# Attention units in another order: the 448- and the 576-column unit of every pair change places

## The chip, the cores and the metric

The kernel runs on one core of one Trainium2 chip. The metric is the device time of one execution in microseconds (us); less is better. TensorE is called PE here, its weight loads PEld, VectorE DVE, ScalarE ACT, GpSimd POOL, and SP is the queue that issues most DMAs.

## The reference

Causal attention with a decay, for 4 batches of 8 heads, 576 tokens and head size 64, and two feed-forward layers behind it (2304 tokens, width 512):

```
scores = scale * q @ k.T                       # per head, 576 x 576
cum    = cumsum(log(clip(f, 1e-4, 1)))
scores = where(causal, -1e9, scores + cum[:, None] - cum[None, :])
attn   = exp(scores - max) / (sum + 1e-9)
x      = attn @ v                              # heads side by side: 2304 x 512
x      = rms_norm(x) * g
x      = (silu(x @ w_gate) * (x @ w_val)) @ w_out    # 512 -> 1536 -> 512
out    = silu(x @ w_in) @ w_out2                     # 512 -> 2048 -> 512
```

## The kernel before

**Units.** The attention runs over 16 pairs of heads (4 batches of 4 pairs). Both heads of a pair sit side by side in 128 partitions. The 576 queries of a pair are cut into nine blocks of 64. Block c, with both heads 128 rows, needs the keys up to its own, (c + 1) * 64 columns; this is a unit of class `Rows` (line 449). So a pair has nine units, of 64 to 576 columns, and `ORDER` (line 33) says in which order they come. All 144 units form one row, and a loop (line 644) walks along it, one step for each unit:

```
if 0 <= s + 1 < N:     units[s + 1].bias()       # POOL
if 0 <= s - TURN < N:  units[s - TURN].turn()    # PE, then ACT or DVE; TURN = 4
if 0 <= s < N:         units[s].scores()         # PE, then DVE
                       units[s].expo()           # ACT
if 0 <= s - USE < N:   units[s - USE].use()      # PE, then ACT; USE = 6
for fn in jobs.pop(s, ()): fn()
```

Position 0 is the first unit of a pair here, position 8 its last. "The turn at position 3" is then the turn of the unit at position 8 of the pair before, since the turn is four steps behind the scores.

**The steps of a unit.** `bias` (line 455) makes the decay row `dt` on POOL; there are six buffers. `scores` (line 463) takes three matmuls (L472: high and low parts) into a PSUM bank of the kind "s", of which there are four, shared in turn with the transposes of the next pair's operands. One DVE instruction (L475) then adds the decay, writes `pr` and takes the extreme `nm`. A bank holds 512 columns, so the unit of 576 columns takes two banks (320 and 256 columns), two L475, and one small DVE instruction more (L482) that joins the two extremes. `expo` (L488) is one exponential on ACT, behind it an instruction that reads the row sum. `turn` (line 491) transposes the probabilities on PE into a bank of the kind "t" (three of them) and moves them to SBUF as `g`. Which engine does that move is said by `ON_ACT = (3, 4, 5, 6, 7, 9, 10, 11)`: unit 6 (448 columns) is moved by ACT, unit 8 (576 columns) by DVE, and unit 8 has one transpose more (L504) with a move of its own, `gl`, on ACT. `use` (L528) multiplies by the values for the whole pair when the step of the pair's last unit comes (`if self.c == ORDER[-1]`).

**Jobs.** During a pair, at fixed positions, the operands of the next pair are made: position 1 loads its decay sums, position 3 transposes its keys (L425, "nk"), position 4 its queries (L425, "nq"), position 5, behind `use`, the tails (L442). Each takes an "s" bank; ACT writes the high part out of it (L273) and DVE the low part (L274), and then the bank is free. At the end of each batch some steps more are there: row sums (L321, L323), the mean of squares (L303, L310), the scale factors (L371, L377, L380).

**Order of the queues.** Each engine works through its own queue in order. The program order above is where the queues start from; the framework's planner orders each queue when the kernel is built, and gives out the banks, by its own idea of when things are ready. While the attention runs, weights of the feed-forward layers are loaded and repacked on ACT (L148) and DVE (L149 to L152). The feed-forward layers (L778) follow.

Of the kernel before, what the change touches and what calls it, by code (L numbers as in the profile page):

```python
# [29 lines left out]

WARM = (12, 1, 2, 5)

ORDER = (0, 1, 7, 2, 6, 3, 5, 4, 8)

TURN = 4
USE = 6
# [26 lines left out]
def block_kernel(ctx: ExitStack, tc: tile.TileContext, q, k, v, f, w_gate, w_val, w_o1, rms_g, w_in, w_o2, ident_d, sel_d, hot_d, out):  # L63
# [150 lines left out]
    def attention():  # L214
        exps, maxima = [], []
        with ExitStack() as st:
# [232 lines left out]
            class Rows:  # L449
# [57 lines left out]
                def use(self):  # L507
                    if self.c == ORDER[-1]:
                        outs = [self.use_group(gi) for gi in range(2)]
                        for out_ in outs:  # L510
                            out_()
# [112 lines left out]
            for n, p in enumerate(pairs):  # L624
                s = n * per
                units += [Rows(p, c) for c in ORDER]
                if n:
# [409 lines left out]
```

## Time and profile before

| | |
|---|---|
| median of 3 runs | 1025.91 us (1025.36 to 1026.23) |
| the profiled execution | 1025.31 us |
| its span, first to last instruction | 1023.5 us |
| busy in the span: PE / PEld / DVE / ACT / POOL | 1011.4 / 847.7 / 761.1 / 566.9 / 401.2 us |
| granted TensorE clock | 1.0 in the whole span (2.4 GHz) |
| attention, to about 216 us | ACT busy 191.58 us, DVE 178.26 us |

A row of a timeline gives start and duration, engine, line, and what is written out of what. Matmuls are pipelined: the duration of one reaches over the start of the next, so that the distance from start to start is what one costs, and a PE that shows as busy may still have room.

### The profile page before, as it was taken

Reading aid. Unit: us, or ns where it says so; the run is one execution under the profiler, and the core shown is the slowest. Engines: PE = TensorE matmul, PEld = TensorE weight load, DVE = VectorE, ACT = ScalarE, POOL = GpSimd, SP = SyncE. Lnnn points to the kernel's source line nnn. Section 1 sums busy time; section 2 is a strip of 40 time slices with the busy share of each in tenths; the row PEclk is TensorE's granted clock in tenths of the full one; section 3 lists DMA queues with packets and bytes.
Section 4 is the critical chain, followed back from the end, with each engine's and each line's share of the span. In section 5 each row is a group of like instructions: output and inputs, shape, how many; then the busy total and the mean of one; then the engine's idle time right before and its main releaser. Section 6 shows DMA issues by size and latency. Waiting matters only on the chain.

```text
span 1023.5 us, 16104 instructions
## 1 busy us (share of the span) xinstructions
PE 1011.4 (99%) x5463; PEld 847.7 (83%) x5463; DVE 761.1 (74%) x1520; ACT 566.9 (55%) x1193; POOL 401.2 (39%) x613
## 2 busy tenths in 40 slices
PE   9999999999999999999999999999999999999998
PEld 7787788878888888888888888888888888888887
DVE  7889887877778797976688768846666696466664
ACT  7998989873444232544544556564444464534441
POOL 8777666511022026331365334435533322222310
PEclk9999999999999999999999999999999999999999
DMA  5764533123544444231334122223322233121102
GB/s 140 193 189 114 126 92 94 27 63 124 185 142 167 159 150 154 73 124 49 106 124 143 64 65 79 83 83 114 113 83 83 83 124 144 42 71 54 52 1 83
DMA packets 114162, 106.40 MB, mean 104 GB/s; under 512 B 62896, under 2 KB 83792, under 8 KB 114080
## 3 DMA queue, kind: packets, MB, share of 16 engines
q1 hardware_dynamic: 112352, 102.23, 32.5%
q10 hardware_dynamic: 1728, 3.15, 1.0%
q8 instruction: 43, 0.70, 0.3%
q14 instruction: 39, 0.32, 0.1%
HBM read 79.59 MB, written 25.76 MB: 103 GB/s over the span
## 4 chain that ended last, share of the span: by engine, by line
PE 77%; DVE 2%; issue 0%; ACT 0%
PE t L778 40%; PE s L778 20%; PE x L778 16%; PE o L528 0%; DVE hl L696 0%; PE s L303 0%; DVE b11l L696 0%; DVE c L912 0%; PE t L497 0%; PE t L528 0%; DVE f L151 0%; DVE ms L342 0%; ACT pr L488 0%; DVE c L152 0%; DVE wl L174 0%
## 5 line engine op out<-in xcount | busy, mean ns | idle before, releaser
L206 POOL TENSOR_TENSOR wol<-c,woh 128x512 fp32r<-128x512 f32 x53 | 78.7, 1491 | 241.8 <-ACT woh L205 218.3
L696 DVE TENSOR_TENSOR hl<-c,hh 128x512 fp32r<-128x512 f32 (+1 forms) x140 | 114.4, 825 | 45.3 <-ACT hh L695 44.4
L167 POOL TENSOR_TENSOR f<-f 128x256 f32<-128x256 f32 x112 | 93.7, 859 | 112.9 <-DMA f<-keptb 51.2
L695 ACT ACTIVATE hh<-c 128x512 fp32r<-128x512 f32 (+1 forms) x140 | 79.7, 582 | 46.3 <-DVE c L912 41.6
L790 ACT ACTIVATE c<-t 128x512 f32<-128x512 f32 x84 | 49.8, 593 | 95.0 <-PE t L778 93.9
L459 POOL TENSOR_SCALAR dt<-ncb,c8t 128x64 f32<-128x64 f32 (+2 forms) x144 | 79.2, 552 | 35.9 <-DVE nm L475 27.5
L488 ACT ACTIVATE pr<-pr,nm 128x192 f32<-128x192 f32 (+3 forms) x144 | 80.2, 558 | 11.6 <-DVE nm L475 8.1
L905 ACT ACTIVATE c<-c 128x512 f32<-128x512 f32 x66 | 41.6, 630 | 80.8 <-DVE c L795 80.8
L475 DVE CUSTOM_DVE_ANT_0 pr<-s,dt 128x256 f32<-128x256 f32 (+7 forms) x160 | 70.1, 450 | 13.4 <-PE t L497 4.8
L193 POOL TENSOR_TENSOR wl<-f,wh 128x1024 fp32r<-128x1024 f32 x12 | 28.8, 2396 | 125.6 <-ACT wh L192 118.9
L497 PE MATMUL t<-ident,pr 128*128 128x128 f32 x384 | 69.2, 279 | 3.7 <-ACT pr L488 2.6
L174 DVE TENSOR_TENSOR wl<-f,wh 128x1024 fp32r<-128x1024 f32 (+1 forms) x48 | 57.7, 1209 | 20.4 <-ACT wh L172 20.2
L795 DVE TENSOR_TENSOR c<-t,c 128x512 f32<-128x512 f32 x60 | 41.1, 687 | 39.4 <-ACT c L790 26.2
L172 ACT ACTIVATE wh<-f 128x1024 fp32r<-128x1024 f32 (+1 forms) x56 | 54.4, 973 | 23.4 <-PE x L778 18.9
L778 PE MATMUL s<-hh,woh 128*128 128x512 f32 (+1 forms) x172 | 64.0, 372 | 0.2 <-DVE xa L959 0.2
L778 PE MATMUL s<-hh,wol 128*128 128x512 f32 (+1 forms) x172 | 64.0, 372 | 0.0
L778 PE MATMUL s<-hl,woh 128*128 128x512 f32 (+1 forms) x172 | 63.9, 372 | 0.0
L977 DVE TENSOR_TENSOR xa<-x,xa 128x512 f32<-128x512 f32 x64 | 43.5, 682 | 25.2 <-PE x L778 25.1
L977 DVE TENSOR_TENSOR xa<-s,xa 128x512 f32<-128x512 f32 (+1 forms) x63 | 42.9, 683 | 25.5 <-PE s L778 25.1
L905 ACT ACTIVATE c<-t 128x512 f32<-128x512 f32 (+1 forms) x74 | 37.9, 512 | 35.9 <-PE t L778 33.8
L148 ACT ACTIVATE f<-st 128x512 f32<-128x512 f32 x42 | 27.8, 668 | 53.6 <-DMA keptb<-f 18.1
L959 DVE TENSOR_TENSOR xa<-s,xa 128x512 f32<-128x512 f32 (+1 forms) x72 | 45.4, 638 | 14.0 <-PE s L778 13.9
(248 smaller groups left out, 3234.1 us busy)
## 6 DMA issues: line engine op xcount, KB each, us to landing
st<-in_moe_w_out_dram SPq DMA_DIRECT2D x28, 512.0 KB, 3.7
st<-in_moe_w_in_dram SPq DMA_DIRECT2D x16, 512.0 KB, 3.8
f<-keptb SPq DMA_DIRECT2D x32, 256.0 KB, 2.6
st<-in_moe_w_gate_dram SPq DMA_DIRECT2D x12, 512.0 KB, 4.2
kepta<-f SPq DMA_DIRECT2D x24, 256.0 KB, 2.3
st<-in_moe_w_val_dram SPq DMA_DIRECT2D x12, 512.0 KB, 4.6
f<-kepta SPq DMA_DIRECT2D x24, 256.0 KB, 2.8
out_dram<-xa SPq DMA_DIRECT2D x17, 256.0 KB, 2.0
```

The lines of the kernel that those rows point to most:

```text
L167: nc.gpsimd.tensor_tensor(out=out_, in0=x, in1=y, op=op)
L174: (nc.gpsimd if plain and i else nc.vector).tensor_tensor(out=lo[i][:, v], in0=f[i][:, v], in1=hi[i][:, v].bitcast(F32), op=ALU.subtract)
L206: nc.gpsimd.tensor_tensor(out=lo, in0=f, in1=hi.bitcast(F32), op=ALU.subtract)
L459: nc.gpsimd.tensor_scalar(out=dt, in0=p.nct[:, 0 if last else D :][:, :n], scalar1=c8t[:, c, p.i : p.i + 1], scalar2=1.0, op0=ALU.add, op1 ...
L475: reduced = nc.vector.tensor_tensor_reduce(out=self.pr[:, ks], in0=sp, in1=self.dt[:, ks], op0=ALU.add, op1=ALU.min, scale=-SCALE, scalar= ...
L488: e = nc.scalar.activation(out=pr, in_=pr, func=AF.Exp, bias=self.nm, scale=-1.0, accum_out=p.batch.sums[:, self.c, p.hp : p.hp + 1])
L497: nc.tensor.transpose(pt[:, jj * P : (jj + 1) * P], keys[:, jj * P : (jj + 1) * P], ident)
L695: nc.scalar.activation(out=hi, in_=src, func=AF.Copy)
L696: nc.vector.tensor_tensor(out=lo, in0=src, in1=hi.bitcast(F32), op=ALU.subtract)
L778: nc.tensor.matmul(ps, lhsT=l, rhs=r, start=start and z == 0, stop=stop and z == len(mms) - 1, skip_group_check=not (start and stop))
L905: act = nc.scalar.activation(out=hf, in_=a, func=AF.Silu)
L977: nc.vector.tensor_tensor(out=a, in0=ps, in1=a, op=ALU.add)
```

## The change

The sixth and the eighth entry of the table are exchanged: unit 8 (576 columns) goes from position 8 to position 4, unit 6 (448 columns) from position 4 to position 8, in all 16 pairs. All else in the text of the kernel stays: `use` comes at the same step, but the last unit ahead of it is now unit 6; and the moves stay with their engines.

```diff
-ORDER = (0, 1, 7, 2, 6, 3, 5, 4, 8)
+ORDER = (0, 1, 7, 2, 8, 3, 5, 4, 6)
```

In columns: before 64, 128, 512, 192, 448, 256, 384, 320, 576; after 64, 128, 512, 192, 576, 256, 384, 320, 448.

## Rows read from the trace of the kernel before

**Rows 1.** Busy time in two stretches: us; PE, PEld, DVE, ACT, POOL (instructions), clock.

```profile
0.00:216.00 216.00, 207.80 (x1621) 171.96 (x1621) 178.26 (x638) 191.58 (x553) 144.15 (x381) 1.00 0.46 116
216.00:1023.50 807.50, 803.61 (x3843) 675.76 (x3843) 582.89 (x883) 375.33 (x641) 257.03 (x232) 1.00 0.31 101
```

**Rows 2.** Waits of PEld (weight loads) to 217 us: total, times, longest.

```profile
PEld t L497 <- ACT pr L488: 8.0, 18, 0.9
```

**Rows 3.** Timeline of PE around the turn at position 3, one pair.

```profile
158.65 0.38 PE L497 MATMUL t<-ident,pr 128*128 128x128 f32 x2
...
160.37 0.39 PE L472 MATMUL s<-op0l,op0h 128*128 128x512 f32 x1
160.60 0.40 PE L472 MATMUL s<-op0h,op0l 128*128 128x512 f32 x1
161.43 0.66 PE L497 MATMUL t<-ident,pr 128*128 128x128 f32 x4 [0.44 <-ACT pr L488]
...
163.97 0.36 PE L472 MATMUL s<-op0h 128*128 128x256 f32 x1
...
169.13 0.60 PE L497 MATMUL t<-ident,pr 128*128 128x128 f32 x4
```

**Rows 4.** The same turn in the first and in the last of the nine pairs where it waits.

```profile
21.53 0.28 PE L472 MATMUL s<-op1l,op1h 128*128 128x192 f32 x1
21.79 0.66 PE L497 MATMUL t<-ident,pr 128*128 128x128 f32 x4
...
186.35 0.25 PE L472 MATMUL s<-op0h 128*128 128x192 f32 x1
186.44 0.28 PE L472 MATMUL s<-op0l,op0h 128*128 128x192 f32 x1
187.03 0.66 PE L497 MATMUL t<-ident,pr 128*128 128x128 f32 x4 [0.32 <-ACT pr L488]
```

**Rows 5.** Timeline of DVE in the stretch of rows 3.

```profile
158.42 0.49 DVE L475 CUSTOM_DVE_ANT_0 pr<-s,dt 128x320 f32<-128x320 f32 x1
...
160.06 0.17 DVE L482 TENSOR_TENSOR nm<-nm 128x1 f32<-128x1 f32 x1
...
162.67 0.69 DVE L280 COPY g<-t 128x512 f32<-128x512 f32 x1
...
164.79 1.28 DVE L274 TENSOR_TENSOR op1l<-s,op1h 128x512 fp32r<-128x512 f32 x2 [0.34 <-ACT op1h L273]
```

**Rows 6.** Timeline of ACT in the same stretch.

```profile
160.18 0.35 ACT L488 ACTIVATE pr<-pr,nm 128x64 f32<-128x64 f32 x1 [0.26 <-DVE nm L475]
...
160.52 0.76 ACT L488 ACTIVATE pr<-pr,nm 128x576 f32<-128x576 f32 x1
161.19 0.19 ACT L488 ACTIVATION_READ_ACCUMULATOR pr<-pr,nm 128x1 f32 x1
```

**Rows 7.** Groups by shape to 270 us: busy us, mean ns.

```profile
L475 DVE CUSTOM_DVE_ANT_0 pr<-s,dt 128x448 f32<-128x448 f32 x16 | 9.9, 619 | 1.8 <-POOL pr L484 0.5 <-ACT pr L488 0.5 <-POOL dt L459 0.4
...
L488 ACT ACTIVATE pr<-pr,nm 128x448 f32<-128x448 f32 x16 | 10.6, 665 | 1.5 <-DVE nm L475 1.5
```

**Rows 8.** Timeline of PE, the second bank of unit 8, first and last of five pairs.

```profile
65.59 0.31 PE L472 MATMUL s<-op0h,op0l 128*128 128x320 f32 x1
66.14 0.35 PE L472 MATMUL s<-op0h 128*128 128x256 f32 x1 [0.24 <-DVE op1l L274]
...
195.93 0.31 PE L472 MATMUL s<-op0h,op0l 128*128 128x320 f32 x1
196.27 0.39 PE L472 MATMUL s<-op0h 128*128 128x256 f32 x1
```

**Rows 9.** Timeline, the unit of 256 columns at position 5 of another pair.

```profile
47.46 0.27 PE L497 MATMUL t<-ident,pr 128*128 128x128 f32 x1
47.53 0.34 DVE L475 CUSTOM_DVE_ANT_0 pr<-s,dt 128x192 f32<-128x192 f32 x1
...
47.94 0.39 PE L472 MATMUL s<-op1h 128*128 128x256 f32 x1 [0.21 <-DVE nm L475]
```

## The prediction

> **What bounds the kernel now.** I read the stretches first: where is PE the limit? Behind 216 us PE is busy 803.6 of 807.5 us, in the attention 207.8 of 216, with ACT at 191.6 and DVE at 178.3 [rows 1]. So the feed-forward part has no room, and the change touches nothing in it: it starts earlier or later by what the attention gains or loses, and no more. In the attention the busy share of PE says little, since durations reach over the next start; there I went by starts. The Trainium skill (Perfetto Trace Analysis, "Identifying the Most-Contended Engine") goes by another row: not matmul busy time, but the share of the weight loads tells how much room TensorE has. By it the estimate of the room would be 216 less 172.0 / 0.837 (the share behind 216 us, 675.8 of 807.5), 10.5 us [rows 1], against 8.2 by matmul busy time; the sum below does not use it.
>
> Second the waits: the largest of the weight loads in the attention is that of turns (L497) for exponentials, 8.0 us in 18 times [rows 2]. Third the timelines, to see which turn that is. In nine of the 16 pairs it is the turn at position 3, that of unit 8 of the pair before. It has the shortest way of all: three units after its own scores, but these are 64, 128 and 512 columns. In the pair shown its scores are issued by 158.65, and the turn could go at 160.60 + 0.23 (the distance of two 512-column matmuls) = 160.83, 2.2 us later. It goes at 161.43: 0.60 us lost [rows 3]. What was late: unit 8 needs two L475 and the joining L482, which stands in DVE's queue behind the small unit and ends at 160.23; then ACT does the exponential of 64 columns first, that of 576 from 160.52, and its row sum is read at 161.38 [rows 5, 6]. The turn follows at once.
>
> By the same subtraction the nine waits are 0.6 three times, 0.5 three times, 0.3 twice and between 0.1 and 0.2 once. In the first pair it is 21.79 - 21.53 = 0.26 less about 0.1 for a matmul of 192 columns (186.44 - 186.35 = 0.09), in the last 187.03 - 186.44 = 0.59 less the same 0.1 [rows 4]. Together 4.1 us. In the other pairs jobs of the batch's end lie between, and nothing waits.
>
> **The change part by part.** No instruction is added or removed: the same matmuls, L475, exponentials, moves and DMAs. What moves is their place.
>
> *Unit 8 leaves the short way.* At position 4 its turn is at position 8, with the units of 256, 384 and 320 columns and `use` between: from 163.97 to the turn at 169.13 in the pair shown, 5.2 us where 2.7 were needed (158.65 to 161.38) [rows 3, 6]. Its wait of 4.1 us in all goes.
>
> *Unit 6 comes onto the short way.* One L475 of 0.62, no L482, an exponential of 0.67 in place of 0.76 [rows 5, 6, 7]. But unit 8's turn is now in the step just ahead of it (position 8), and DVE's copy of 0.69 belongs to that turn [rows 5]. If the copy comes first: L475 of the 320-column unit ends with its read at about 159.0, the copy to 159.6, L475 of unit 6 to 160.2 with the read, the exponential with its row sum (0.67 + 0.19 from 160.52 to 161.38, less the 0.1 for a shorter row: about 0.8) to 160.95. The turn could go at 160.83, so 0.1 us stays. If the copy comes behind, nothing stays. I take 0.1 in nine pairs: 0.9 us back. The bounds are 0 and 0.3 (if ACT again does the 64-column exponential first, 0.35 [rows 6], of which 0.1 lies beside).
>
> *The second bank of 576 columns.* At position 8 it waits in five pairs: 66.14 - 65.59 = 0.55, where a 320-column matmul costs 0.14 (0.23 of rows 3 times 320/512), so 0.41; the last of the five 0.34 - 0.14 = 0.20 [rows 8]. The five make 1.5 us (0.4, 0.4, 0.2, 0.2, 0.2). There unit 6 takes one bank, and the next is asked for a whole unit later: 1.5 us go.
>
> *Banks at positions 4 and 5.* There one bank more is wanted, next to the keys' (position 3) and the queries' (position 4), which are held longest: the keys' is free only when DVE has made the low part, at about 165.4, while the 256-column unit wants a bank at 163.97 [rows 3, 5]. Rows do not show unit 8 there, so I bound it. From below: nothing. The first bank of unit 8 is read as soon as its matmuls end if DVE is not behind; it takes 0.5, and PE's second half (0.12 a matmul by the same scale, three of them) and the queries' transposes lie between, some 0.8. DVE is less behind there, since the copy of 0.69 at 162.67 [rows 5] has left position 3. From above: the wait for the keys' bank, 165.4 - 163.97 = 1.4 us in each of 15 pairs, 21 us. The nearest row is the same unit at the same place, waiting for a DVE instruction that stands behind weight work: 47.94 - 47.46 less 0.03 for a transpose, 0.45 us [rows 9]. Such waits of some 0.45 are there in four pairs already. I take 0.2 us in eight pairs (those in which DVE repacks weights), 1.6 us, because 0.45 is for a DVE that is behind and nothing for one that is not.
>
> *What costs nothing.* The move of unit 6 (ACT) goes to position 3, that of unit 8 (DVE, and ACT's `gl`) to position 8: `use` needs them only two steps later, and ACT's queue there loses `gl` and gains some 0.3 us; the keys' high part comes later by that, under `use`. Without that cover it is in the 21 us above. POOL prepares each `dt` ahead in six buffers, so its 576-column row at another step is covered by the five units before it; without that it would be the 0.1 us by which that row is longer. SP's loads stay at their steps. Of the three "t" banks unit 8 still takes two in one step, and two engines still free them, DVE's copy and ACT's `gl`. The last pair's tail (no later scores to hide behind) I take at nothing, between -0.5 and +0.5: one L475 less, but the copy ahead of it.
>
> Sum: -4.1 - 1.5 + 0.9 + 1.6 = -3.1 us on the profiled execution's 1025.31 (span 1023.5 and 1.8 around it), which stands 0.6 below the median of 1025.91. From the median: **1022.8 us**. The feed-forward part passes it on.
>
> **The rivals.**
> A. *The gain goes to another wait; no change.* ACT is busy 89% of the attention and DVE 83% [rows 1]. In pairs with a batch's end or weight work a PE that comes earlier may only wait for a bank a step later. Against it: the nine waits are caused by an order of queues, not by a lack of engine time, and DVE and ACT stand in that order because unit 8 has more steps than any other [rows 5, 6]. If 4 of the 5.6 us come back so: -1.6 us, 1024.3. 0.26.
> B. *The bank at position 5; slower.* If the 256-column unit gets the keys' bank, or unit 8's L475 stand behind the keys' low part on DVE (0.65 each, half of rows 5's 1.28), it waits 0.65 us in 15 pairs: +9.8 - 5.6 + 0.9 = +5.1, 1031.0. It decides from (5.6 - 0.9) / 15 = 0.3 us a pair. For it: four waits there already [rows 9]. Against it: in rows 8 the wanted bank is not always the one given out longest ago, and in rows 4 the plan has pulled matmuls of the next unit ahead of a late turn; `use` could be pulled ahead likewise. The Trainium skill (the same page, "Optimization Strategy") says that a gap that repeats on the engine that should be full can mean that there is no PSUM for the next tile; rows 8 agree, and by that rule the change carries the gap from position 8 to position 4 or 5 and this rival is what it gives. 0.19.
> C. *The change does all at no cost:* -4.1 - 1.5 - 0.5 (tail) = -6.1, 1019.8: the good end of the forecast.
>
> **How the numbers follow.** Forecast (with C) 0.55, A 0.26, B 0.19. About 0.2%, 2 us, is what a measurement tells from no change. Forecast: faster; A: -1.6 lies inside, as part of the forecast's own spread does, and as part of A's spread lies beyond it. So faster 0.55, same 0.26, slower 0.19. The forecast's own range is 1019.5 to 1024. For 8 in 10 I reach from just under C, 1019.0, into B: the milder half of it, 1030.0.
>
> **What the profile would show.** Right: the L497 of position 3 starts within 0.25 us of the last 512-column matmul, and PEld's wait of turns for exponentials falls from 8.0 to about 4 us; no second bank waits at position 8; the feed-forward part, behind 216 us before, starts some 3 us earlier. A step is wrong if PE waits at position 3 as before (then the copy stands ahead and ACT's order is bad), or if L472 of 256 columns or the second bank of unit 8 waits for DVE L274 or L475 in most pairs (B). The prediction as a whole is wrong if the stretch behind the attention changes its own length by more than 1 us.

## The result, and the profile after

The changed kernel takes 1039.87 us (median of 4 runs, 1039.49 to 1040.61), the kernel before on the same chip 1025.63: 14.2 us more, ratio 1.014 with a 95% interval of 1.0127 to 1.0153. The forecast was 1022.8, in a range from 1019.0 to 1030.0. It went the way of rival B, and further than its price.

The stretches of the kernel after; columns as in [rows 1].

```profile
0.00:230.50 230.50, 214.89 (x1621) 171.84 (x1621) 184.03 (x639) 192.62 (x553) 145.24 (x381) 1.00 0.43 110
230.50:1038.50 808.00, 803.43 (x3843) 675.92 (x3843) 582.37 (x882) 374.52 (x641) 256.43 (x232) 1.00 0.31 100
```

The same 1621 matmuls of the first stretch take 230.5 us in place of 216, with the same weight-load time (171.8 against 172.0): nothing became dearer, there are only more gaps. The second stretch is 808.0 against 807.5 [rows 1]. The whole loss lies in the attention, at a granted clock of 1.00.

The waits of the kernel after, first of PEld to 232 us (the rows that answer to [rows 2]), then one of ACT from 18 to 222 us.

```profile
PEld t L497 <- ACT pr L488: 5.9, 14, 0.8
PEld s L472 <- DVE nm L475: 5.2, 13, 0.8
PEld t L504 <- ACT g L278: 4.7, 6, 1.5
PEld s L425 <- DVE nm L475: 3.2, 6, 0.8
```
```profile
ACT pr L488 <- DVE nm L482: 6.0, 11, 1.3
```

Two rows of the kernel before, from 18 to 222 us:

```profile
PEld s L472 <- DVE nm L475: 3.0, 8, 0.5
ACT pr L488 <- DVE nm L482: 0.7, 2, 0.4
```

Turns wait less for exponentials, 5.9 us where it was 8.0 [rows 2], as forecast in its direction. But scores and operands (L472, L425) wait for DVE to read banks, 8.4 us together where L472 alone had 3.0; unit 8's fifth transpose (L504) waits for ACT's moves; and ACT itself stands 6.0 us in 11 times with unit 8's exponential at the head of its queue, waiting for the joining L482.

One pair shows how these hang together. Position 4 in the kernel after, DVE's timeline:

```profile
134.23 0.49 DVE L475 CUSTOM_DVE_ANT_0 pr<-s,dt 128x320 f32<-128x320 f32 x1 [0.29 <-ACT pr L488]
134.65 0.08 DVE L475 DVE_READ_ACCUMULATOR2_ANT nm<- 128x1 f32 x1
...
135.56 0.69 DVE L274 TENSOR_TENSOR op0l<-s,op0h 128x512 fp32r<-128x512 f32 x1 [0.83 <-ACT op0h L273]
...
136.17 0.41 DVE L475 CUSTOM_DVE_ANT_0 pr<-s,dt 128x256 f32<-128x256 f32 x1
...
136.51 0.29 DVE L280 COPY g<-t 128x128 f32<-128x128 f32 x1
...
136.71 0.19 DVE L482 TENSOR_TENSOR nm<-nm 128x1 f32<-128x1 f32 x1
```

The same stretch on PE, then on ACT:

```profile
134.12 0.28 PE L472 MATMUL s<-op1h,op1l 128*128 128x256 f32 x1
...
135.24 0.66 PE L425 MATMUL s<-ident,nq 128*128 128x128 f32 x4
...
136.40 0.36 PE L472 MATMUL s<-op1h 128*128 128x256 f32 x1 [0.51 <-DVE op0l L274]
```
```profile
134.03 0.58 ACT L278 ACTIVATE g<-t 128x512 f32<-128x512 f32 x1
134.51 0.45 ACT L488 ACTIVATE pr<-pr,nm 128x192 f32<-128x192 f32 x1
134.85 0.19 ACT L488 ACTIVATION_READ_ACCUMULATOR pr<-pr,nm 128x1 f32 x1
134.95 0.58 ACT L273 ACTIVATE op0h<-s 128x512 fp32r<-128x512 f32 x1
135.93 0.59 ACT L273 ACTIVATE op0h<-s 64x512 fp32r<-64x512 f32 x1 [0.40 <-PE s L425]
137.02 0.78 ACT L488 ACTIVATE pr<-pr,nm 128x576 f32<-128x576 f32 x1 [0.50 <-DVE nm L482]
```

Unit 8's second half is in its bank at 134.4. DVE, done with the first half at 134.7, has the low part of the keys (L274) next in its queue. That needs ACT's high part, and ACT comes to it only at 134.95, behind a move and an exponential. So DVE stands for 0.83 us, works 0.6 on the keys, and reads the second half from 136.17: its bank is held some 1.4 us longer than DVE's work on unit 8 asks for. The 256-column unit starts at 136.40, and the row names what it waited for: not unit 8's bank, which is still being read, but the one that L274 lets go, the keys'. The exponential starts at 137.02, 2.6 us behind its scores. In the trace an L274 stands between unit 8's two L475 in 7 of 16 pairs, and in 8 more between them and the join alone; in the kernel before in none, since at position 8 no keys or queries are near.

That pair is not the common case of PE's waits for "s" banks. Position 4 of another pair, DVE, then PE:

```profile
91.42 0.57 DVE L353 SCALAR_TENSOR_TENSOR z<-z,ms 128x5 f32<-128x5 f32 x1
92.03 0.17 DVE L355 SCALAR_TENSOR_TENSOR y<-z,y 128x5 f32<-128x5 f32 x1
92.17 0.36 DVE L475 CUSTOM_DVE_ANT_0 pr<-s,dt 128x192 f32<-128x192 f32 x1
...
93.71 0.69 DVE L274 TENSOR_TENSOR op1l<-s,op1h 128x512 fp32r<-128x512 f32 x1
94.31 0.15 DVE L482 TENSOR_TENSOR nm<-nm 128x1 f32<-128x1 f32 x1
```
```profile
92.59 0.66 PE L425 MATMUL s<-ident,nq 128*128 128x128 f32 x4 [0.55 <-DVE nm L475]
```

Unit 8 has taken two banks, so the queries (L425) wait until the 192-column unit's is read. DVE reads it late, and not for ACT: it is behind with scale factors of the batch's end. The L274 comes after both halves and delays the join alone. Of the 19 waits of L472 and L425 for L475 listed above, 11, together 5.9 of the 8.4 us, end at an L475 that DVE reached late in this way, without a pause, behind steps of a batch's end or the repacking of weights.

What was forecast of position 3 and position 8 came true. PE of the kernel after, the turn at position 3:

```profile
171.35 0.39 PE L472 MATMUL s<-op0l,op0h 128*128 128x512 f32 x1
171.58 0.40 PE L472 MATMUL s<-op0h,op0l 128*128 128x512 f32 x1
171.87 0.66 PE L497 MATMUL t<-ident,pr 128*128 128x128 f32 x4
```

It starts 0.29 behind the last 512-column matmul, 0.06 above what a matmul of that size takes, where it was 0.60 above [rows 3]. The turn at position 8, however, has a gap of its own now; PE, then ACT:

```profile
179.79 0.60 PE L497 MATMUL t<-ident,pr 128*128 128x128 f32 x4
181.68 0.30 PE L504 MATMUL t<-ident,pr 128*64 128x128 f32 x1 [1.30 <-ACT g L278]
```
```profile
181.03 0.60 ACT L278 ACTIVATE g<-t 128x512 f32<-128x512 f32 x1
```

The fifth transpose wants a second "t" bank, and the one that comes free is unit 7's, which ACT moves only at 181.03.

### The profile page after: what moved, and what is told of

Read it like the earlier page. It is cut to its first block, busy times and chain, and to the rows that moved or that the text cites. A ratio compares the mean times of both kernels' runs of the same rounds, so it can differ in the third digit from the quotient of the medians.

```text
span 1038.5 us, 16113 instructions
## 1 busy us (share of the span) xinstructions
PE 1018.3 (98%) x5463; PEld 847.8 (82%) x5463; DVE 766.4 (74%) x1520; ACT 567.1 (55%) x1193; POOL 401.7 (39%) x613
## 4 chain that ended last, share of the span: by engine, by line
PE 83%; ACT 5%; DVE 4%; issue 1%; DMA 1%; POOL 0%; SPq 0%; ACTq 0%; DVEq 0%
PE t L778 39%; PE s L778 20%; PE x L778 16%; PE s L472 2%; ACT pr L488 2%; PE o L528 2%; PE t L497 2%; ACT g L278 1%; DVE pr L475 1%; PE t L528 1%; DMA st<-in_moe_w_in_dram 0%; DVE r L321 0%; PE s L303 0%; PE s L377 0%; ACT op0h L273 0%
## 5 line engine op out<-in xcount | busy, mean ns | idle before, releaser
L696 DVE TENSOR_TENSOR hl<-c,hh 128x512 fp32r<-128x512 f32 (+1 forms) x140 | 116.7, 842 | 45.0 <-ACT hh L695 44.2
L488 ACT ACTIVATE pr<-pr,nm 128x64 f32<-128x64 f32 (+2 forms) x144 | 80.1, 557 | 19.8 <-DVE nm L475 13.1
L475 DVE CUSTOM_DVE_ANT_0 pr<-s,dt 128x256 f32<-128x256 f32 (+7 forms) x160 | 70.4, 449 | 14.8 <-PE t L497 4.9
```

The lines of the kernel that those rows point to most:

```text
L475: reduced = nc.vector.tensor_tensor_reduce(out=self.pr[:, ks], in0=sp, in1=self.dt[:, ks], op0=ALU.add, op1=ALU.min, scale=-SCALE, scalar= ...
L488: e = nc.scalar.activation(out=pr, in_=pr, func=AF.Exp, bias=self.nm, scale=-1.0, accum_out=p.batch.sums[:, self.c, p.hp : p.hp + 1])
L696: nc.vector.tensor_tensor(out=lo, in0=src, in1=hi.bitcast(F32), op=ALU.subtract)
```

## The experiments

Three theories were set against each other as the runs went on. S: five "s" banks are wanted at positions 4 and 5, and there are four. T: at position 8 unit 8 takes two of three "t" banks. Q, later Q': the queues of DVE and ACT are in a worse order; Q' names the place, the keys' L274 within unit 8's DVE steps. Each time is given with its distance from the kernel before in the same series (1025.25 to 1025.54); the changed kernel stands at +14.2.

**The banks, by way of the "o" bank.** This is the one bank of a third kind; only `use`, at position 5, asks for it. L504's target and the second half's target are changed, alone and together, and together in the order of before:

```diff
-pt = bank(pst)                 # fifth transpose of unit 8
+pt = bank(pso)
...
-sp = bank(pss)[:, :w]          # scores
+sp = bank(pso if n > SF and k0 else pss)[:, :w]
```

> The changed order, but the fifth transpose of unit 8 (L504) writes to the 'o' bank, which is idle at that step, in place of a second 't' bank. Theory T (at position 8 unit 8 asks for two of three t banks right behind the turns of units 7 and 2, and PE waits until ACT has moved unit 7): 4.2 us of waits of L504 go and some of the turns behind it, so 1033 to 1035 us. Theory S (the fifth scores bank wanted at positions 4 and 5 is the loss): within 1 us of the changed kernel's 1039.9. Theory Q (the queues of ACT and DVE are in a worse order, banks only show it): no change, 1039 to 1040.

> The changed order, but the second half of unit 8's scores goes to the 'o' bank in place of a second 's' bank, so that positions 4 and 5 ask for as many s banks as before the change. Theory S: the waits of L425 (2.2 us), of the 256-column matmuls and of unit 8's two halves (some 6 us together) go, 1031 to 1034 us. Theory T: 1039 to 1040. Theory Q: 1039 to 1040.

> The changed order with both: second half of unit 8's scores and its fifth transpose in the 'o' bank. If the whole loss is banks (T and S together), 1024 to 1028 us, the time of before or below it. Theory Q: above 1036. T alone 1033 to 1035, S alone 1031 to 1034.

> The order of before with the same two edits. They take away the waits of the second half at position 8 (1.2 to 1.5 us), and nothing else is known to wait for these banks there: 1024.0 to 1025.6 us by S and T alike; Q expects 1025.6.

Fifth transpose: 1038.79 (+13.5). Second half: 1032.80 (+7.5). Both: 1031.89 (+6.6). Control: 1025.55 (+0.2, interval of the ratio 0.9991 to 1.001). T brings 0.8 us and falls as the main cause, although its wait was the longest single gap: with the second "t" bank out of the way the lateness shows elsewhere, PEld's wait of turns for exponentials to 232 us going from 5.9 to 9.3 us. S brings 6.8, about half. Where the rest went is seen in the waits of the run with both, from 18 to 222 us:

```profile
PEld o L528 <- DVE nm L475: 5.6, 10, 1.2
...
ACT pr L488 <- DVE nm L482: 4.2, 7, 1.0
```

Now `use` waits for the "o" bank until DVE has read unit 8's second half, up to 1.2 us: the bank is still read late. That turned the question from how many banks to what DVE does in between.

**Queries and tails one step later.**

```diff
-WHEN = dict(load=-12, k=-6, sums=-8, q=-5, tails=-4)
+WHEN = dict(load=-12, k=-6, sums=-8, q=-4, tails=-3)
```

> The changed order with all banks as they were, but the next pair's queries are transposed one step later (position 5, behind use, in place of position 4) and its tails at position 6, so that only the keys share the s banks with unit 8's two halves and the 256-column unit. Theory S (too many s banks wanted at positions 4 and 5): a gain like that of the second half in the o bank, without its cost to use: 1029 to 1033 us. Theory Q (the order of work on ACT and DVE, whatever the banks): 1039 to 1040, since the same work comes only 4 us later.

> The order of before with queries and tails one step later, the control. S expects next to nothing, since positions 4 and 5 have only some 0.8 us of bank waits to lose: 1024.5 to 1026. If the later step is of use for another reason, it is faster here too, by several us.

> The changed order with queries and tails one step later and unit 8's fifth transpose in the o bank. S with T as the second cause: 2 to 4 us under the run with the later queries alone. S alone, the t banks being only where a late ACT shows: within 1 us of it.

1047.81 (+22.3) in the changed order, 1043.50 (+18.0) in the order of before, 1046.39 (+20.9) with the fifth transpose in the "o" bank. All missed what was expected: the later step costs 18 us by itself, for a reason that I did not follow up, so the runs do not tell S from Q. Only this much: with the queries elsewhere the two orders lie 4.3 us apart, not 14.2.

**The keys' L274 out of unit 8's way.** Keys behind unit 8's scores (k=-5) or one step ahead (k=-7), or unit 8's DVE steps given priority when the queue is planned; and the keys behind the unit of position 4 in the order of before:

```diff
-WHEN = dict(load=-12, k=-6, sums=-8, q=-5, tails=-4)
+WHEN = dict(load=-12, k=-5, sums=-8, q=-5, tails=-4)     # the other run: k=-7
```
```diff
+with tc.high_priority(offset=AHEAD) if n > SF else ExitStack():
     reduced = nc.vector.tensor_tensor_reduce(...)        # L475
...
+with tc.high_priority(offset=AHEAD):
     nc.vector.tensor_tensor(out=nms[0], in0=nms[0], in1=nms[1], op=ALU.min)   # L482
```

> The changed order; the next pair's keys are transposed behind the scores of unit 8 (position 4, ahead of the queries) in place of position 3. Theory Q' (at position 4 DVE's queue has the low part of the keys, L274, which waits for ACT, between unit 8's two L475 or ahead of the joining L482; unit 8's exponential and, behind it on ACT, all moves come late, and the second bank stays held): in this kernel's DVE queue no L274 stands between unit 8's first L475 and its L482 in any pair (in the changed kernel one does in most), so 6 to 12 us of the 14 come back, 1028 to 1034. Theory S (the number of s banks asked for at positions 4 and 5, wherever DVE's queue stands): the same five banks are asked for within the same two steps, so 1038 to 1041.

> The changed order, where unit 8's L475 and L482 have priority over other ready work in the planning of DVE's queue. No L274 stands between the two L475 any more, but one still stands ahead of L482 in 13 of 16 pairs, since L482 is not ready at once. Q': part of it comes back, 2 to 6 us, 1034 to 1038: the bank is free earlier, the exponential is not. If the bank held by the second half is all of it: 1031 to 1034.

> The changed order; the keys one step earlier (position 2, behind the 512-column unit). L274 of the keys then stands behind the 512-column unit's L475, none between unit 8's two, and ahead of L482 mostly a small copy. Q': 1028 to 1034 if ACT makes the high part in time, less if DVE now waits for ACT ahead of the 192-column unit. S: 1036 to 1040 (the keys' bank comes free a little earlier).

> The order of before with the keys behind unit 6 at position 4, the control for the run with the keys behind unit 8. Q' expects little, since unit 6 has one L475 and nothing that L274 could split: 1024.5 to 1027. If keys behind the scores are better or worse for a reason of their own, it shows here.

Keys behind: 1031.38 (+6.1). Priority: 1034.24 (+9.0). Keys earlier: 1037.62 (+12.3). Control: 1026.33 (+1.1). The first is the plain case for Q': the same banks are asked for within the same steps, and 8.1 us come back with DVE reading unit 8 at once. Its DVE, the same place in a pair:

```profile
129.12 0.49 DVE L475 CUSTOM_DVE_ANT_0 pr<-s,dt 128x320 f32<-128x320 f32 x1
...
129.54 0.42 DVE L475 CUSTOM_DVE_ANT_0 pr<-s,dt 128x256 f32<-128x256 f32 x1
...
130.00 0.16 DVE L482 TENSOR_TENSOR nm<-nm 128x1 f32<-128x1 f32 x1
130.84 0.69 DVE L274 TENSOR_TENSOR op0l<-s,op0h 128x512 fp32r<-128x512 f32 x1 [0.68 <-ACT op0h L273]
```

The two halves and the join follow each other (129.12 to 130.16; 134.23 to 136.90 in the changed kernel), and DVE's wait for ACT, still 0.68, comes behind them. Moving the keys also changes the order in which banks are asked for, unit 8's two now ahead of the keys'. The priority edit touches DVE's steps alone; it leaves no L274 between the halves, but one ahead of the join in 13 pairs, and brings 5.3 us. So DVE's queue counts without any change in the requests. Which part of it counts most, the held bank or the late exponential, is not shown. Waits of the keys behind, from 18 to 222 us:

```profile
PEld s L425 <- DVE nm L475: 4.2, 9, 0.9
PEld s L472 <- DVE nm L475: 3.7, 8, 0.8
PEld t L504 <- ACT g L278: 3.0, 6, 1.0
...
ACT pr L488 <- DVE nm L482: 3.3, 5, 1.1
```

The waits for banks that DVE reads are as long as in the changed kernel (7.9 us against 7.7 in this stretch); those for ACT's moves and of ACT for the join are shorter, 3.0 us where it was 4.7 and 3.3 where it was 6.0. That speaks for the late exponential as what this edit gives back, and is no test.

Keys earlier is the run that went against Q': 1.9 us, in the range that S gave. No L274 stands between unit 8's halves there and one ahead of the join in 4 pairs only, so a queue of DVE that is clear around unit 8 is not enough. Its waits to 232 us name another place:

```profile
PEld s L425 <- DVE op0l L274: 2.4, 4, 1.1
PEld s L472 <- DVE op0l L274: 2.4, 2, 1.3
PEld s L425 <- DVE op1l L274: 2.3, 5, 0.5
```

Queries and the 256-column unit now wait for L274 itself to let a bank go, 7.1 us in all. This was read from the waits and not tested.

**All three together, and other places for unit 8.** First the keys behind with both "o" edits, in both orders; then two more orders, with the kernel otherwise as before:

```diff
+ORDER = (0, 1, 7, 2, 6, 3, 5, 8, 4)     # 576 at position 7
+ORDER = (0, 1, 7, 2, 6, 3, 8, 4, 5)     # 576 at position 6
```

> The changed order with the keys behind unit 8 (no L274 between its halves) and with its second half and its fifth transpose in the o bank. If DVE's queue (Q') and the banks (S, T) are the whole loss, the time of before, 1024.5 to 1027. If a part of the loss is that unit 8 stands at position 4 at all (its long DVE and ACT steps next to those of keys and queries, whatever queue and bank), 1029 to 1032.

> The order of before with the same three edits, the control: 1025 to 1027.5, from the +1.0 that the keys behind cost and the +0.2 that the o bank cost here.

> Another order: units 4 and 8 of the order before exchanged (576 columns at position 7, 320 last), all else as before. No key, query or tail job is near, and no L274 stands between unit 8's halves in any pair; the last unit is short. If the loss comes from position 4 (Q', S), this is no slower than before, and the short way that unit 8 leaves gives its 2 to 4 us: 1021.5 to 1025. If T (two t banks at once right behind unit 7's turn) were a cause of its own, it shows less here, since the turn stays behind small units. If taking unit 8 from the last position is what costs, 1028 or more.

> Unit 8 at position 6, 320 at position 7, 384 last. Here the tails' short L274 (0.28 each) stands between unit 8's halves in 11 of 16 pairs. Q': a smaller loss than with the keys' L274, in all 1025 to 1031; if only the keys' and queries' banks count (S), 1022 to 1025; if taking unit 8 from the last position costs, 1028 or more as at position 7.

Changed order with the three edits: 1025.68 (+0.3, ratio 1.0003, 0.9994 to 1.0012). The 14.2 us are back. Its control, the order of before with the same edits: 1023.53 (-1.9, ratio 0.9983, 0.9974 to 0.9993), the fastest version of all, and below the 1025 to 1027.5 that was expected. Under equal edits the changed order still costs 2.2 us; what those are I did not settle.

Unit 8 at position 7: 1032.60 (+7.2); at 6: 1032.49 (+7.1). By Q' and S the first should have been no slower than before, and both lie where they were expected "if taking unit 8 from the last position is what costs". No key or query is near position 7, and its waits, from 18 to 222 us, are others:

```profile
PEld t L497 <- ACT pr L488: 10.2, 15, 1.1
PEld s L472 <- DVE nm L475: 4.2, 13, 0.6
PEld t L497 <- POOL pr L484: 2.5, 3, 0.8
```

With 320 columns last and unit 8 just ahead of it, turns wait for exponentials 10.2 us, 2.2 more than before, scores for DVE 1.2 more, and turns for POOL (L484) 2.5. So the loss is not one of position 4 alone: as the kernel stands, of the four places tried, the last is the best for unit 8. At position 7 no L274 stands within unit 8's steps, so Q' is not the cause there. What holds the exponentials at 6 and 7 was not tested, and whether part of it acts at position 4 too stays open.

**Which bank.** The keys behind, with one "o" edit at a time:

> The changed order with the keys behind unit 8 (1031.4 by itself) and its second half in the o bank, the fifth transpose in a t bank as in the changed kernel. If the last 5.7 us between that run and the one with all three edits (1025.7) are the s bank: 1026 to 1028. If they are the t banks: 1030 to 1032.

> The same with the fifth transpose in the o bank and the second half in an s bank. If the last 5.7 us are the s bank: 1029.5 to 1031.5; if they are the t banks: 1026 to 1028. If neither edit alone brings more than half of the 5.7, the two banks hold each other up.

Second half: 1026.46 (+1.2). Fifth transpose: 1029.87 (+4.6). From +6.1 the "s" bank brings 4.9, the "t" bank 1.5. The "s" bank brought 6.8 and the keys 8.1 each by itself, and together they bring 13.0: two edits whose gains overlap little.

## Why the prediction was wrong

*Unit 8 leaves the short way; unit 6 comes onto it.* Right. By the prediction's own subtraction the nine turns at position 3 that were 4.1 us late together are 1.4 late, where 0.9 was to stay. PEld's wait of turns for exponentials fell by 2.1 us, to 5.9 in place of the "about 4" that was to be seen, so turns elsewhere wait more than they did. The feared copy cost nothing to speak of in the pair shown.

*The second bank at position 8.* Right: no second bank waits there any more.

*Banks at positions 4 and 5.* This is the step that failed. It was put as "The first bank of unit 8 is read as soon as its matmuls end if DVE is not behind", and priced at 0.2 us in eight pairs, 1.6 us. In its place the runs show 13.0 us: that much comes back when the second half has a bank of its own and the keys stand behind unit 8. Two things were wrong. DVE is behind, in the way of [rows 9]: the 11 waits behind its own work make 5.9 us, 0.5 each and not 0.2. And L274 of the keys stands within unit 8's steps in 15 of 16 pairs; DVE waits there for ACT, and with it the join, the exponential and ACT's moves. For a late exponential the step had no term at all. How the 13.0 us divide between the two is not shown. The upper bound, 21 us, held it; the value was taken near the wrong end, and the range left that end out. The row that would have told of the second was in the rows, the L274 with its idle time for ACT [rows 5]: I read when it ends, and only rival B had it ahead of something urgent. B's sign came: in 10 of the 16 pairs PE waits there for DVE with a 256-column matmul.

*What costs nothing.* "Of the three "t" banks unit 8 still takes two in one step" was right as a count and wrong as a price. At position 3 the turns just ahead are those of units 5 and 4, three transposes each; at position 8 they are those of unit 7, four transposes whose 512 columns ACT has to move, and of unit 2, two. By the runs it cost 0.8 to 1.5 us, though PEld's wait for it is 4.7.

*Rivals.* B was the right place with the right sign, and its price of 0.65 us a pair took one L274 and not the wait inside it: 14.2 us and the gains of some 4 make more than 1 us a pair. The Trainium skill's rule on gaps that repeat (Perfetto Trace Analysis, "Optimization Strategy"), cited there, held by half: 4.9 to 6.8 us came with a bank of its own; 8.1 came with no bank more, by another order of the work. A is refuted by the time: it had no change. Nor did ACT and DVE run out of room, with 192.6 and 184.0 us busy in 230.5, smaller shares than before. The sign that would have made the prediction wrong as a whole did not come: the stretch behind the attention kept its length within 0.5 us.

## What to carry to other kernels

Where a piece of work is moved, ask for each engine what its queue holds next to it at the new place, and above all which neighbour there waits for a third engine: in an in-order queue such a neighbour lends its wait to all behind it, and a unit that needs two steps on that engine can be split by it. Moving the neighbour only helps where its wait does not hold up something else, as the two places for the keys show (8.1 and 1.9 us back). A bank's price is how long it is held, and that is set by all that stands ahead in its reader's queue, the reader's own work too. A wait that is long in the list can be worth little: the one with the longest single gap here, 1.5 us, gave back 0.8 us in all when it was taken away.

## What was not expected of the hardware

Nothing of the chip itself. TensorE's granted clock stayed at 1.00 (2.4 GHz) in the attention of the changed kernel in spite of its added gaps, the longest 1.3 us by PE's row; only in the profiles of the three runs with the queries later was the mean over the span 0.998.
